# An FFT long-convolution layer and an MLP on one core: the second MLP weight loaded behind the first gate, unpadded tables in the first stage for ssm_k, and another order of GpSimd's first work

## The chip, the cores and the metric

The kernel runs on one core of a Trainium2 chip. The time is the device time of one execution in microseconds (us). The engines are TensorE (PE; its weight loads are shown as PEld), VectorE (DVE), ScalarE (ACT), GpSimd (POOL) and SyncE (SP), which here only issues transfers. ScalarE issues a few transfers as well. The core has 16 DMA engines.

## The reference

```python
# B, S, D, Dff, ks = 1, 2048, 512, 1376, 4; bf16 inputs
def _A_ref(q, k, v, shift_k, ssm_k, ssm_D):          # gated long convolution
    k_pad = jnp.pad(k, ((0, 0), (ks - 1, 0), (0, 0)))
    for t in range(ks):                              # 4 taps along the tokens
        k_shift = k_shift + k_pad[:, t:t + S, :] * shift_k[:, ks - 1 - t]
    kv = k_shift * v
    y_f = rfft(pad(kv, 2 * S)) * rfft(pad(ssm_k, 2 * S))     # along the tokens
    y = irfft(y_f)[:S].astype(bfloat16)
    y = y + kv * ssm_D
    return q * y

def _B_ref(x, w1, w2):                               # MLP
    h = jnp.maximum(jnp.einsum("bsd,df->bsf", x, w1), 0)
    return jnp.einsum("bsf,fd->bsd", h, w2)

x = A_q
h = x + _A_ref(_layernorm(x), A_k, A_v, A_shift_k, A_ssm_k, A_ssm_D)
return h + _B_ref(_layernorm(h), B_w1, B_w2)
```

## The kernel before

The order of every engine's instructions is the order in which the program writes them (`tc.manual_schedule()`); waits are put in by the framework where one instruction needs another's data or buffer. The program has two halves.

**The convolution.** The transform over the tokens is done as two stages of matmuls with tables of sines and cosines that the kernel makes itself. `to_rows` transposes `ssm_k` (tile `sk`) into `kfl` with 64 TensorE transposes. Then, in eight rounds `gb`, `taps` multiplies `k` by diagonal matrices `wdiag` (one block of four taps for each 128 channels, `rg` = 0 to 3; round `gb` uses blocks `2 * (gb % 2)` and the next) and VectorE multiplies by `v`; and `stage1(kfl, a1k, gb, ...)` does a part of the first stage for `ssm_k`. `stage1` has two forms. With `pairs=True` (only `gb == 2` for `kfl`) a matmul takes 64 rows and all 128 columns of the padded tables `f2hi`, `f2lo`. Otherwise it takes 32 rows and 64 columns. The table is kept as a high and a low bf16 part: `f1hi`, `f1lo` are 64 columns wide; `f2hi`, `f2lo` are 128 wide and hold in each block of 32 rows the same 64 columns, alternately left and right, with zeros beside them. GpSimd makes the `wdiag` blocks (L229), `f1hi` and `f1lo` (L231 to L233) and the padded copies (L237), then negated tables `c2n` (L240). The same `stage1` later works on `xfl`, the transform of `kv`. The second stage, the product of the two transforms and the first stage of the inverse (`inv1`) follow; the span is then at about 115 us.

**The gate and the MLP.** The 2048 tokens are four groups `q` of 512, each with two halves `h`. `lift(q)` transposes x into `xT[q]` and `ln1_norm(q)` normalises it and transposes it into `qT[q]`, both by DMA transposes on SyncE's queue. `inv2(q, h, ...)` is the last stage of the inverse transform: 64 matmuls with 32 rows each, into a PSUM tile `pz`. `gate(q, h)` on VectorE multiplies `pz` by `qT` (L602, which frees `pz`), adds `xT` (L605), and has SyncE transpose the result back to `xh` (L607). The pool `psz` has one `pz` buffer, so the next `inv2` from it waits for the L602 of the gate before it; `psz0` has a second one at the start only. `mlp1(sc)` makes the hidden layer of a group: 11 blocks `fc` of 4 matmuls with `w1`, each followed by a ReLU on ScalarE into `h1T`. `mlp2(sc)` has four blocks of 11 matmuls with `w2` (tile `w2`, shown as `w` in the profile, like `w1`), each followed by an addition on VectorE and the output's transfers. Hooks put further `half(q, h)` calls (an `inv2` and a `gate`) between these blocks: `half(1, 1)` behind the first block of `mlp2(0)`, `half(2, 0)` behind the third.

`w2` is loaded by `load_w2()`, two DMAs from ScalarE's queue (L681, 1280 KB, and L683, 96 KB). It is called in the hook of `mlp1(0)` at `fc == 1`, so ScalarE issues it behind its second ReLU. The tile lies in a pool that is opened at L593, after `inv1`.

The order at the start of the second half is: `inv2(0, 0)`, `inv2(0, 1)`, `gate(0, 0)`, `inv2(1, 0)`, `gate(0, 1)`, `lift(2)`, `ln1_norm(1)` (which makes `qT[1]`), the wrap of some table arguments, `ln1_stats(2)`, `gate(1, 0)`, `mlp1(0)`, `lift(3)`, `stats(xh[0])`, `ln1_norm(2)`, `mlp2(0)`.

Of the kernel before, what the change touches and what calls it, by code (L numbers as in the profile page):

```python
# [9 lines left out]
ALU = mybir.AluOpType  # L10
# [5 lines left out]
P = 128  # L16
# [40 lines left out]
def kernel(  # L57
# [13 lines left out]
    nc = tc.nc  # L71
    _, S, D = A_q.shape
    DFF = B_w1.shape[1]
# [114 lines left out]
    for a, t in cs:  # L188
        ks = slice(a, a + t.shape[1])
        nc.vector.tensor_tensor(out=tsn[:, ks, :], in0=ta[:, ks].unsqueeze(2).to_broadcast([P, t.shape[1], 64]),  # L190
                                in1=ta[:, 32:96].unsqueeze(1).to_broadcast([P, t.shape[1], 64]), op=ALU.add)
# [7 lines left out]
    f1f = early.tile([P, 64], F32, name="f1_f")  # L199
# [21 lines left out]
    f1hi = early.tile([P, 64], BF16, name="f1_hi")  # L221
    f1lo = early.tile([P, 64], BF16, name="f1_lo")
    f2hi = consts.tile([P, P], BF16, name="f2_hi")
    f2lo = consts.tile([P, P], BF16, name="f2_lo")
# [3 lines left out]
    for rg in range(DC):  # L228
        nc.gpsimd.tensor_tensor(out=wdiag[:, rg, :, :], in0=ident[:].unsqueeze(1).to_broadcast([P, KS, P]),  # L229
                                in1=wsh[:, rg, :].unsqueeze(2).to_broadcast([P, KS, P]), op=ALU.mult)  # L230
    nc.gpsimd.tensor_copy(out=f1hi[:, 0:64], in_=f1f[:])  # L231
    nc.gpsimd.tensor_tensor(out=f1f[:], in0=f1f[:], in1=f1hi[:, 0:64], op=ALU.subtract)
    nc.gpsimd.tensor_copy(out=f1lo[:, 0:64], in_=f1f[:])  # L233
    for f, g in ((f1hi, f2hi), (f1lo, f2lo)):
        for rg in range(DC):
            rows = slice(32 * rg, 32 * rg + 32)
# [1 line left out]
    for a, b in ((0, 8), (8, 16), (16, 22), (22, 24), (24, 32)):  # L238
        (ao, to), (ai, ti) = [[p for p in tab if p[0] <= a][-1] for tab in (cn, cs)]
        nc.gpsimd.tensor_single_scalar(out=to[:, a - ao:b - ao, :], in_=ti[:, a - ai:b - ai, :].bitcast(F32), scalar=-1.0,  # L240
                                       op=ALU.mult)

    def copy(eng, o, i):
        if eng == "A":
            nc.scalar.copy(out=o, in_=i)  # L245
        else:
            nc.vector.tensor_copy(out=o, in_=i)
# [9 lines left out]
    def bank2(name):  # L257
        return place([P, 2, 512], F32, name)
# [11 lines left out]
    def stage1(fl, a_out, gb, engs, pairs=False):  # L270

        pss = [bank2("ps1") for _ in range(2)]
        n, tabs = 2 if pairs else 4, (f2hi, f2lo)
        K = P // n
        for gi in range(8):
            for f in range(2):
                for t in range(n):
                    rows = slice(K * t, K * t + K)
                    cols = slice(0, P)
                    if pairs:  # L280
                        o = pss[t][:, gi // 4, 128 * (gi % 4):128 * (gi % 4) + 128]
                    else:
                        cols = slice(64 * (t % 2), 64 * (t % 2) + 64)
                        o = pss[t // 2][:, t % 2, 64 * gi:64 * gi + 64]
                    nc.tensor.matmul(out=o, lhsT=fl[rows, 8 * gb + gi, :, :].rearrange("p d n -> p (d n)"),  # L285
                                     rhs=tabs[f][rows, cols], start=(f == 0), stop=(f == 1),
                                     tile_position=(K * t, 0), skip_group_check=True)
        for h in range(2):
            if pairs:
                src = pss[h][:].rearrange("p b (g r c) -> p c (b g) r", g=4, r=2)  # L290
            else:
                src = pss[h][:].rearrange("p r (g c) -> p c g r", c=64)
            dst = a_out[:, :, 32 * gb:32 * gb + 32].rearrange("p c (g r) -> p c g r", r=DC)[:, :, :, 2 * h:2 * h + 2]
            for g, eng in enumerate(engs[h]):
                n = 8 // len(engs[h])
                copy(eng, dst[:, :, g * n:g * n + n], src[:, :, g * n:g * n + n])
# [12 lines left out]
    kfl = early.tile([P, 64, 2, 64], BF16, name="kfl")  # L309
# [26 lines left out]
    for gb in range(8):  # L336
        taps(gb // 2, gb % 2)
        stage1(kfl, a1k, gb, ("AA", "AD")[gb % 2], pairs=(gb == 2))
        if gb in (0, 1, 3, 5):
            cc_part()  # L340
# [21 lines left out]
    for q in range(8):  # L362
# [4 lines left out]
        if "DADDADAD"[q] == "D":  # L367
            nc.vector.tensor_single_scalar(out=xfl32[:, :, :, ms],
                                           in_=pst[:].bitcast(I32).rearrange("p m (d g) -> p g d m", d=2),
# [23 lines left out]
    for gb in range(8):  # L393
        stage1(xfl, a1x, gb, ("A", "DA" if gb == 4 else "D"), pairs=(gb > 0))
# [114 lines left out]
    def ec_sins(q):  # L509
        for h, t in ((0, ecs[q % 2]), (1, ecr[q % 2])):  # L510
            _sin(ecore[q][:, h, :, :].rearrange("p j n -> p (j n)"), t, 8192, neg=(h == 1))
# [83 lines left out]
    w2 = mp.tile([P, NFC, D], BF16, name="w2")  # L595
# [4 lines left out]
    def gate(q, h):  # L600
        ii = slice(2 * h, 2 * h + 2)
        nc.vector.tensor_tensor(out=qT[q][:, ii].rearrange("p i r t -> p r i t"),  # L602
                                in0=pzs[q, h].rearrange("p r (i a) n -> p r i (a n)", i=2),
                                in1=qT[q][:, ii].rearrange("p i r t -> p r i t"), op=ALU.mult)
        nc.vector.tensor_tensor(out=xT[q][:, ii], in0=qT[q][:, ii], in1=xT[q][:, ii], op=ALU.add)  # L605
        hT[q] = xT[q]
        nc.sync.dma_start_transpose(out=xh[q][:, ii].rearrange("p i (r c) -> p (i r) c", r=DC),  # L607
                                    in_=hT[q][:, ii].rearrange("p i r t -> p (i r) t"))

    def inv2(q, h, pool, width=4):  # L610
        pz = pool.tile([P, DC, 512], F32, tag="pz", name="pz")[:]
        pzs[q, h] = pz[:, :, 0:256].rearrange("p r (j n) -> p r j n", n=32)
        for jl in range(8):
            j = 8 * h + jl
            n2 = 16 * (j % 4) + 4 * q + j // 4
            w = min(width, 16 - j)
            for rho in range(2):
                for rg in range(DC):
                    rows = slice(32 * rg, 32 * rg + 32)
                    nc.tensor.matmul(out=pz[:, rg, 32 * jl:32 * (jl + w)],  # L620
                                     lhsT=ax[rows, 64 * rho + n2, :, :].rearrange("p d g -> p (d g)"),
                                     rhs=ecore[q][rows, rho, j:j + w, :].rearrange("p a b -> p (a b)"),
                                     start=(rho == 0), stop=(rho == 1), tile_position=(32 * rg, 0), skip_group_check=True)
# [40 lines left out]
    pl.pop("psIb")  # L664
    psz = pl.push("psZ", space=PSUM)
    psz0 = pl.push("psZ0", space=PSUM)
    inv2(0, 0, psz, 8)
    inv2(0, 1, psz0, 8)
    gate(0, 0)
    inv2(1, 0, psz, 8)  # L670
    gate(0, 1)
    pl.pop("psZ0")
# [3 lines left out]
        inv2(q, h, psz)  # L676
        gate(q, h)

    def load_w2():
        nfull = DFF // P  # L680
        nc.scalar.dma_start(out=w2[:, 0:nfull, :], in_=B_w2[0:nfull * P, :].rearrange("(c p) d -> p c d", p=P))  # L681
        if DFF % P:
            nc.scalar.dma_start(out=w2[0:DFF % P, nfull, :], in_=B_w2[nfull * P:DFF, :])  # L683

    def in_mlp1_0(fc):
        if fc == 1:
            load_w2()
        if fc in (6, 8):
            ec_sins(2 + (fc - 6) // 2)

# [18 lines left out]
    ln1_stats(2)  # L709
    gate(1, 0)  # L710
    mlp1(0, in_mlp1_0)
    lift(3)
    stats(xh[0], mv2, rstd2, 0)
# [44 lines left out]
```

## Time and profile before

| What | Value |
|---|---|
| time, median of 5 runs | 218.22 us (217.30 to 219.06) |
| time of the profiled execution | 217.86 us |
| its span | 216.1 us |
| mean granted TensorE clock | 0.991 |
| TensorE busy | 196.4 us, 91% of the span |
| VectorE, ScalarE, GpSimd busy | 144.3, 116.3, 79.1 us |
| w2's larger DMA (1280 KB), issue to landing | 9.9 us |
| w1's DMA (1376 KB), issue to landing | 6.0 us |

In the profile, times count from the start of the span. A line of the timeline gives start, duration, engine, source line, operation, output and inputs, the number of instructions, and in brackets how long the engine sat idle before it and what ended that. A line of the chain of waits gives start, duration and what was running, traced back from the last instruction. "Granted clock" is the share of full speed that TensorE's clock was given in a stretch. The profiled execution's own time is 1.8 us more than its span.

### The profile page before, as it was taken

What the parts mean: (1) busy time and instruction counts of PE and PEld (TensorE: products, weight loads), DVE (VectorE), ACT (ScalarE), POOL (GpSimd) and SP (SyncE); (2) the same over time, 40 slices, a digit from 0 to 9 for tenths busy, and PEclk for the clock granted to TensorE, in tenths of its full rate; (3) what the DMA queues carried; (4) which work ended last, traced back from release to release, by engine and by line L of the source; (5) the groups of instructions that cost most, each with busy time, mean ns of one, the idle gap of its engine ahead of it and who ended that gap; (6) DMA issues with size and microseconds to landing.
All of it is one profiled execution on the core that took longest, in us unless ns stands there. A gap on an engine that the chain in (4) does not pass through costs nothing.

```text
span 216.1 us, 5476 instructions
## 1 busy us (share of the span) xinstructions
PE 196.4 (91%) x2267; PEld 137.0 (63%) x2267; DVE 144.3 (67%) x238; ACT 116.3 (54%) x178; POOL 79.1 (37%) x120
## 2 busy tenths in 40 slices
PE   0399999999987999999998995999999999999992
PEld 0395546999766999979997642554646644444451
DVE  7997778766887998986969940987395470243031
ACT  2967988755894888886991275002450047016400
POOL 3299992000016999977678020010202010002000
PEclk9999999999999999999999998899999999999999
DMA  6999950000000017549630599494454430010012
GB/s 188 310 223 187 156 129 10 2 0 3 3 3 2 3 46 182 228 111 200 113 67 3 104 265 189 75 188 88 92 88 86 97 73 3 24 49 24 0 48 53
DMA packets 49513, 20.08 MB, mean 93 GB/s; under 512 B 44400, under 2 KB 47952, under 8 KB 49488
## 3 DMA queue, kind: packets, MB, share of 16 engines
q1 hardware_dynamic: 47360, 18.24, 40.6%
q10 hardware_dynamic: 2128, 1.48, 2.8%
q8 instruction: 18, 0.29, 0.5%
q14 instruction: 7, 0.06, 0.1%
HBM read 7.08 MB, written 2.10 MB: 42 GB/s over the span
## 4 chain that ended last, share of the span: by engine, by line
PE 75%; DMA 10%; DVE 8%; ACT 3%; issue 1%; SPq 0%; DVEq 0%; ACTq 0%
PE ps2m L649 19%; PE ps1m L632 14%; PE pkv L328 7%; PE psy L435 6%; DMA w<-in_B_w_dram 5%; PE pz L620 4%; PE ps L285 4%; DMA sk<-in_A_ssm_k_dram 4%; PE ps2k L303 3%; PE ps2k L305 3%; PE u L303 3%; PE pst L267 3%; PE u L305 3%; PE psi L562 3%; DVE st L515 2%; PE pst L365 2%
## 5 line engine op out<-in xcount | busy, mean ns | idle before, releaser
L634 ACT ACTIVATE h1T<-ps1m 128x512 bf16<-128x512 f32 (+1 forms) x44 | 25.8, 596 | 60.0 <-PE ps1m L632 59.9
L649 PE MATMUL ps2m<-w,h1T 128*128 128x512 bf16 (+3 forms) x187 | 41.1, 378 | 2.3 <-DMA w<-in_B_w_dram 2.3
L632 PE MATMUL ps1m<-xT,w 128*128 128x512 bf16 (+1 forms) x176 | 38.8, 379 | 0.4 <-DVE xT L605 0.4
L652 DVE SCALAR_TENSOR_TENSOR o<-ps2m,rstd,xh 128x512 bf16<-128x512 f32 (+1 forms) x17 | 12.1, 718 | 31.2 <-PE ps2m L649 29.0
L649 PEld LDWEIGHTS <-h1T 128*128 128x128 bf16 (+1 forms) x187 | 18.2, 100 | 23.0 <-DMA w<-in_B_w_dram 2.7
L632 PEld LDWEIGHTS <-w 128*128 128x128 bf16 (+1 forms) x176 | 17.4, 100 | 20.7 <-DVE xT L605 0.6
L425 POOL TENSOR_TENSOR t<-usb,kf 128x320 fp32r<-128x320 f32 x32 | 28.2, 945 | 2.4 <-ACT usb L421 2.1
L425 DVE TENSOR_TENSOR t<-u,kf 128x704 fp32r<-128x704 f32 x32 | 26.7, 889 | 3.4 <-ACT usb L421 3.4
L519 POOL TENSOR_SCALAR rstd<-mv 128x4 f32<-128x4 f32 x8 | 2.3, 283 | 71.5 <-DVE mv L517 71.5
L602 DVE TENSOR_TENSOR qT<-pz,qT 128x1024 bf16<-128x1024 f32 x8 | 9.7, 1218 | 15.0 <-DMA qT<-qln 8.4
L515 DVE BATCH_NORM_STATS2 st<-xh 128x6 f32<-128x512 bf16 x32 | 19.7, 677 | 0.0
L245 ACT CAST kf<-psy 128x512 fp32r<-128x512 f32 x30 | 17.6, 646 | 1.9 <-PE psy L435 0.2
L620 PEld LDWEIGHTS pz<-ecore,ax 32*128 32x128 f32 x512 | 15.0, 186 | 3.1 <-issue 1.3
L620 PE MATMUL pz<-ecore,ax 32*128 32x128 f32 (+7 forms) x512 | 15.7, 273 | 0.7 <-DVE wm L550 0.7
L435 PE MATMUL psy<-t,ipos 128*128 128x512 f32 x48 | 16.0, 394 | 0.0
L562 PE MATMUL psi<-dre,kf 128*128 128x256 f32 x64 | 15.5, 285 | 0.0
L562 PE MATMUL psi<-dim,kf 128*128 128x256 f32 x64 | 15.3, 281 | 0.0
L328 PE MATMUL pkv<-kT,wdiag 128*128 128x512 bf16 x64 | 15.2, 381 | 0.0
L267 PE MATMUL pst<-ident,sk 128*128 128x128 bf16 x64 | 6.7, 297 | 9.1 <-DMA sk<-in_A_ssm_k_dram 9.1
L331 DVE TENSOR_TENSOR sk<-pkv,vT 128x512 bf16<-128x512 f32 x16 | 10.9, 690 | 5.5 <-PE pkv L328 5.5
L245 ACT CAST a1k<-ps 128x1024 fp32r<-128x1024 f32 x12 | 12.6, 1093 | 3.4 <-PE ps L285 3.4
L245 ACT CAST ax<-psi 128x1024 fp32r<-128x1024 f32 x13 | 12.4, 1017 | 3.0 <-PE psi L562 2.9
(116 smaller groups left out, 389.2 us busy)
## 6 DMA issues: line engine op xcount, KB each, us to landing
sk<-in_A_ssm_k_dram SPq DMA_DIRECT2D x1, 2048.0 KB, 8.4
xh<-in_A_q_dram SPq DMA_DIRECT2D x16, 128.0 KB, 3.2
out_dram<-o SPq DMA_DIRECT2D x60, 32.0 KB, 1.6
w<-in_B_w_dram SPq DMA_DIRECT2D x1, 1376.0 KB, 6.0
w<-in_B_w_dram ACTq DMA_DIRECT2D x1, 1280.0 KB, 9.9
xh<-xT SPq DMA_TRANSPOSE x8, 3.1
w<-in_B_w_dram ACTq DMA_DIRECT2D x1, 96.0 KB, 9.8
kT<-in_A_k_dram SPq DMA_TRANSPOSE x4, 6.6
```

The costliest lines, as they stand in the source:

```text
L245: nc.scalar.copy(out=o, in_=i)
L267: nc.tensor.transpose(out=pst[:, i, :], in_=src[:, :, :, 8 * q + i], identity=ident[:])
L303: nc.tensor.matmul(out=ps[:, kk, :], lhsT=at_k1(w_re, k1), rhs=a_in[:, k1, :], start=True, stop=False, skip_group_check=True)
L328: nc.tensor.matmul(out=pss[i][:], lhsT=wdiag[:, 2 * h + i, j, :], rhs=kT[c][:, 2 * h + i, 16 - j:CH + 16 - j], start=(j == 0), stop=(j == ...
L425: eng.tensor_tensor(out=t[:, :, j, :], in0=in0.unsqueeze(1).to_broadcast([P, 2, n, 2]), in1=kfr[:, :, j, ks], op=ALU.mult)
L435: nc.tensor.matmul(out=psy[:], lhsT=m_[:], rhs=t_.rearrange("p j k -> p (j k)"), start=first, stop=not first)
L515: nc.vector.bn_stats(out=st[:, i, :], in_=src[:, i, :])
L562: nc.tensor.matmul(out=ps[:, i // 2, i % 2, :], lhsT=kf[:, c, 4 * m:4 * m + 4, :].rearrange("p r k -> p (r k)"), rhs=d[:].rearrange("p d a ...
L620: nc.tensor.matmul(out=pz[:, rg, 32 * jl:32 * (jl + w)], lhsT=ax[rows, 64 * rho + n2, :, :].rearrange("p d g -> p (d g)"), rhs=ecore[q][ro ...
L632: nc.tensor.matmul(out=ps1[:fsz, :].rearrange("p (i t) -> p i t", i=4), lhsT=w1[:, c, fc * P:fc * P + fsz], rhs=hT[sc][:, :, c, :], start= ...
L634: nc.scalar.activation(out=h1T[:fsz, fc, :], in_=ps1[:fsz, :], func=ACT.Relu)
L649: nc.tensor.matmul(out=ps2[:, 0:w], lhsT=h1T[:ksz, fc, i * P:(i + 1) * P], rhs=w2[:ksz, fc, ds], start=(fc == 0), stop=(fc == NFC - 1))
```

## The change

Three edits. First, GpSimd makes `f1hi` and `f1lo` after the second of the four `wdiag` blocks and not after the fourth. Second, `stage1` for `kfl` reads `f1hi` and `f1lo` in its form without pairs; the form with pairs, and both forms for `xfl`, read `f2hi` and `f2lo` as before. Third, `load_w2()` is called right behind `gate(0, 0)`, after a new VectorE memset of one column in each of `w2`'s 11 chunks (128 partitions x 11 elements). The load writes over that column, so its DMA waits for the memset, and the memset stands on VectorE behind the two operations of `gate(0, 0)` and ahead of those of `gate(0, 1)`. The call in the hook of `mlp1(0)` is gone.

```diff
     for rg in range(DC):
         nc.gpsimd.tensor_tensor(out=wdiag[:, rg, :, :], in0=ident[:].unsqueeze(1).to_broadcast([P, KS, P]),
                                 in1=wsh[:, rg, :].unsqueeze(2).to_broadcast([P, KS, P]), op=ALU.mult)
-    nc.gpsimd.tensor_copy(out=f1hi[:, 0:64], in_=f1f[:])
-    nc.gpsimd.tensor_tensor(out=f1f[:], in0=f1f[:], in1=f1hi[:, 0:64], op=ALU.subtract)
-    nc.gpsimd.tensor_copy(out=f1lo[:, 0:64], in_=f1f[:])
+        if rg == 1:
+            nc.gpsimd.tensor_copy(out=f1hi[:, 0:64], in_=f1f[:])
+            nc.gpsimd.tensor_tensor(out=f1f[:], in0=f1f[:], in1=f1hi[:, 0:64], op=ALU.subtract)
+            nc.gpsimd.tensor_copy(out=f1lo[:, 0:64], in_=f1f[:])
...
-        n, tabs = 2 if pairs else 4, (f2hi, f2lo)
+        n, tabs = 2 if pairs else 4, (f2hi, f2lo) if pairs or fl is not kfl else (f1hi, f1lo)
...
-                        cols = slice(64 * (t % 2), 64 * (t % 2) + 64)
+                        if fl is not kfl:
+                            cols = slice(64 * (t % 2), 64 * (t % 2) + 64)
+                        else:
+                            cols = slice(0, 64)
...
     inv2(0, 0, psz, 8)
     inv2(0, 1, psz0, 8)
     gate(0, 0)
+    nc.vector.memset(w2[:, :, 0:1], 0.0)
+    load_w2()
     inv2(1, 0, psz, 8)
     gate(0, 1)
...
     def in_mlp1_0(fc):
-        if fc == 1:
-            load_w2()
         if fc in (6, 8):
             ec_sins(2 + (fc - 6) // 2)
```

More of the change, by code (lines that the diff above doesn't have):

```diff
@@ L666, with load_w2 @@
     psz0 = pl.push("psZ0", space=PSUM)
+    def load_w2():
+        nfull = DFF // P
+        nc.scalar.dma_start(out=w2[:, 0:nfull, :], in_=B_w2[0:nfull * P, :].rearrange("(c p) d -> p c d", p=P))
+        if DFF % P:
+            nc.scalar.dma_start(out=w2[0:DFF % P, nfull, :], in_=B_w2[nfull * P:DFF, :])
     inv2(0, 0, psz, 8)
@@ L677, in half @@
         gate(q, h)
[L679 to L683, printed above, removed]
     def in_mlp1_0(fc):
-        if fc == 1:
-            load_w2()
         if fc in (6, 8):
```

## The prediction

> **What bounds the kernel now.** I read the page first: TensorE (PE) is busy for most of the span, so only its gaps can be won.
>
> ```profile
> span 216.1 us, 5476 instructions
> PE 196.4 (91%) x2267; PEld 137.0 (63%) x2267; DVE 144.3 (67%) x238; ACT 116.3 (54%) x178; POOL 79.1 (37%) x120
> ```
>
> Then the chain of waits in order of time, around the load that is moved:
>
> ```profile
> 120.75 0.70 DVE xT L605
> ...
> 121.50 1.91 PE ps1m L632 x8
> ...
> 123.44 9.95 DMA w<-in_B_w_dram
> ...
> 133.44 4.24 PE ps2m L649 x11
> 137.68 1.89 PE pz L620 x61
> ```
>
> The reader is to see that a transfer sits in the chain: w2 is asked for at 123.44, behind two ReLUs, lands 9.95 us later, and TensorE's first second-layer block (11 matmuls) starts at once. Third, the timeline of TensorE there:
>
> ```profile
> 121.50 9.67 PE L632 MATMUL ps1m<-xT,w 128*128 128x512 bf16 x44 [0.43 <-DVE xT L605]
> 133.44 4.24 PE L649 MATMUL ps2m<-w,h1T 128*128 128x512 bf16 x11 [2.27 <-DMA w<-in_B_w_dram]
> ...
> 146.30 2.55 PE L649 MATMUL ps2m<-w,h1T 128*128 128x512 bf16 x11
> ```
>
> The gap is 2.27 us, and the block behind it takes 4.24 us where the same 11 matmuls take 2.48 in the chain at 146.37. The table of stretches (TensorE busy, then its granted clock, DMA share, GB/s) says why:
>
> ```profile
> 61.96:65.37 3.41, 2.07 (x63) 1.00 0.00 0
> ...
> 130.23:133.64 3.41, 1.14 (x6) 1.00 1.19 165
> 133.64:137.05 3.41, 3.41 (x9) 0.50 0.32 72
> ```
>
> After a stretch of 3.41 us in which TensorE worked 1.14 us, it got half clock for the next 3.41 us. After one with 2.07 busy (1.35 idle) it did not. So w2's lateness costs 2.27 + (4.24 - 2.48) = 4.03 us. Fourth, who else waits on a transfer: the timeline of VectorE (DVE) and of SyncE's queue (SPq).
>
> ```profile
> 118.89 0.69 DVE L605 TENSOR_TENSOR xT<-qT,xT 128x1024 bf16<-128x1024 bf16 x1
> 119.50 1.22 DVE L602 TENSOR_TENSOR qT<-pz,qT 128x1024 bf16<-128x1024 f32 x1
> ...
> 135.18 1.23 DVE L602 TENSOR_TENSOR qT<-pz,qT 128x1024 bf16<-128x1024 f32 x1 [8.45 <-DMA qT<-qln]
> ```
>
> ```profile
> 119.61 3.09 SPq L607 DMA_TRANSPOSE xh<-xT  x2
> 122.81 1.90 SPq L523 DMA_TRANSPOSE xT<-xh  x1
> 124.80 7.38 SPq L523 DMA_TRANSPOSE qT<-qln  x1
> ```
>
> gate(1, 0) at 135.18 waits for the transpose qT[1], issued at 124.80 and landed 10.3 us later, at 135.1. inv2(1, 1) needs the PSUM tile that this gate frees at 135.18 + 1.23 = 136.41. Now that hides behind the slow block, which ends at 137.68. It is what is late next.
>
> **The change part by part.**
>
> *GpSimd's order and the unpadded tables.* No instruction is added. The first stage for ssm_k issues as many matmuls of 64 columns, on f1 instead of f2, and TensorE's order is the same.
>
> ```profile
> 9.44 4.91 POOL L229 TENSOR_TENSOR wdiag<-ident,wsh 128x512 bf16<-128x512 bf16 x4 [6.27 <-DMA wsh<-in_A_shift_k_dram]
> ...
> 16.32 1.09 POOL L237 COPY f_lo<-f_lo 32x64 bf16<-32x64 bf16 x4
> ```
>
> The padded copies end at 16.32 + 1.09 = 17.41. TensorE's first stage-1 matmul is at 17.50, straight behind its taps (chain: 15.84 + 1.73 = 17.57), so it waits for nothing. After: two wdiag blocks end near 9.44 + 4.91/2 = 11.9 (f1's sines end at 10.41), hi and lo take 0.94 (14.29 to 15.23 now) to 12.85, the other two wdiag blocks end near 15.3 and are first needed at 18.11: 2.8 us of cover. The padded tables still end at 17.4, but are first needed at the paired third block, at 22.40. Value taken: 0. A later wsh could make it a gain of a few tenths in a run; a loss needs 2.8 us.
>
> *The memset.* One DVE instruction more, 128x11, between gate(0, 0) and gate(0, 1). This trace has none of its strided form; its nearest rows are memsets of 0.06 us (128x1) and 0.09 us (128x32). I take 0.1, ends 0.05 and 0.2. It is on the path: mlp1(0) starts when gate(0, 1) ends, so TensorE ends mlp1(0) at 131.17 + 0.1 = 131.27.
>
> *The load's two issues* leave ScalarE (ACT) behind the second ReLU (0.38 + 0.97 us) and run near 119.7 to 121.1, when the memset has ended. ScalarE is idle from 114.99 to 122.58, so the wait added on its queue delays only what starts at 122.58: nothing. The last ReLU of mlp1(0), at 132.7 because two pairs of sines of 1.3 us come before it, is needed by the block's eleventh matmul, at 131.27 + 10 x 0.216 = 133.4.
>
> *The load itself* starts 3.7 us earlier. From issue to landing it took 9.95 us among transposes; w1, of the same 1376 KB, took 6.0 us without company. So it lands between 125.7 and 129.7, and is needed at 131.27: 1.5 us of cover even at the worse end. The block then ends at 131.27 + 2.48 = 133.75 instead of 137.68. Were this all, the gain is 3.9 us.
>
> *What the load is moved past:* on the 16 DMA engines, most of the first xh transpose, the second, xT[2] and qT[1]. They take turns with it packet for packet (queue 10 is w2's, queue 1 the transposes'):
>
> ```profile
> q10 hardware_dynamic: 271, 0.28, 79.8%
> q1 hardware_dynamic: 270, 0.07, 31.3%
> ```
>
> That is the microsecond from 126; alone, queue 1 moved 808 packets from 121 to 122. So the xh and xT[2] transposes come later, but their readers have room (stats of xh[0] at 137.05, gate(2, 0) at 146.4). qT[1] is last in queue 1 before and after, so it lands when the same total work is done. Only empty time can be saved: 0.4 us at 122.3 to 122.6 with nothing queued, which w2 now fills, and two stalls with work queued, 0.45 us at 129.1 to 129.6 and 1.2 us from 130.75:
>
> ```profile
> DMA packets 18, 0.01 MB, mean 11 GB/s; under 512 B 9, under 2 KB 18, under 8 KB 18
> ```
>
> (the microsecond from 131). The long stall follows an instruction fetch (queue 8) that runs from 129.98 on; the fetch at 20.04 was followed by the same dip, 36 packets in 0.6 us from 21.4. It may well return. So qT[1] lands between 135.1 - 0.4 - 1.65 = 133.1 (no stall) and 134.7 (both). I take 134.0, near the middle.
>
> *Sum.* inv2(1, 1) starts at landing + 0.05 + 1.23 + 0.05 = landing + 1.33: 135.35 instead of 137.68, a gain of 2.3 with TensorE idle for 135.35 - 133.75 = 1.6 us. The next place, inv2(2, 0), needs gate(1, 1), which VectorE frees 143.22 - 135.13 = 8.1 us after the landing; TensorE is there at landing + 1.33 + 1.89 + 4.86 = 8.08: no more than 0.1 lost. Behind it TensorE is the bound again. Total -2.2. The profiled execution (span 216.1, time 217.86, so 1.8 lies around the span) would be 215.7. The median of the runs is 0.36 higher at 218.22: 216.0.
>
> *A rule against the row.* The half clock after 1.14 busy in 3.41 us is weighed against the Trainium skill, "TensorE: Matmul & The Clock Gate", section "Why this matters for your kernels": it asks for no idle gaps above about 3 us, since a whole idle window is what drops the clock. By that rule 2.27 us would cost only itself, removing it while adding 1.6 would be worth 2.27 - 1.6 - 0.1 = 0.6 us, and the new gap could not cost clock. This trace shows the drop after 2.27 us of idling inside one stretch, so I use 4.03. By the trace the new gap has a price as well: idling above a point between 1.35 and 2.27 us in a stretch (1.8 by the middle) costs another 1.75 us.
>
> **The rivals.**
> - *Full gain:* both stalls vanish and qT[1] lands by 132.4. For: the last packets move faster once w2 is out of the way (867 packets from 133 to 134 against 541 at 126). Against: the total work. 218.2 - 3.9 = 214.3.
> - *The new wait turns cold:* qT[1] lands at 134.2 to 135.1; TensorE idles 1.8 to 2.7 us and may get half clock. With the drop: 136.35 - 134.7 - 1.75 = -0.1, so about 218.2; without it 216.6. For: the long stall can return. Against: the stretches run on a fixed grid, which may split the gap.
> - *Slower:* taking turns with w2 from the start makes queue 1 so late that qT[1] lands after 135.7, when the clock loss exceeds what is left of the gain by over 1.1 us. At 136.2: 136.35 - 136.2 - 1.75 = -1.6, so 219.8. For: turns cost queue 1 two thirds of its rate for about 5 us. Against: it gets that back when w2 is done.
> - *Nothing:* w2 does not start earlier, or the wait is exchanged one for one: 218.2. Against: ScalarE is idle at 119.7.
>
> **How the numbers follow.** A warm gap of up to 1.8 us, gain 2.1 to 3.9: 0.50; full gain 0.12; the later landing 0.23 (0.10 warm, 0.13 cold); slower by more than 1.1 us 0.08; nothing 0.07. About 0.5% (1.1 us) is what a measurement here can tell from no change. Faster: 0.50 + 0.12 + 0.10 = 0.72; same: 0.13 + 0.07 = 0.20; slower: 0.08. The range goes from 213.9 (full gain, with 0.4 for the front and for the run) to 218.5 (cold, plus 0.3); the warm case alone would be 214.3 to 216.2.
>
> **What would show it.** Right: w2 issued near 119.7 and landed before 130; ps2m behind ps1m without a gap; its 11 matmuls in 2.5 us; then a wait of inv2(1, 1) of about 1.6 us for gate(1, 0), which itself waits for qT. The front's rows up to 17.5 unchanged. Wrong: qT landed after 134.7 or half clock behind the new gap; TensorE waiting for wdiag at 18.1; or w2 landing after 131.

## The result and the profile after

The changed kernel runs in 217.02 us (median of 20 runs, 215.39 to 219.32) against 218.31 us for the one before (39 runs, 216.41 to 221.33). The ratio is 0.9925, with a 95% interval of 0.9901 to 0.995: about 1.6 us faster (1.1 to 2.2). Four of the 20 runs, at 219 us and with a mean granted clock of 0.979 to 0.984, lie over 1.5% above the fastest and are left out of the ratio; the median of the other 16 is 216.7 us, and no trace shows one of the four. The profiled execution took 217.20 us with a span of 215.4 us; before it was 217.86 and 216.1.

The chain of waits around the load now reads (start, duration, what was running):

```profile
121.86 6.23 PE ps1m L636 x28
...
128.85 5.05 DMA qT<-qln
...
133.99 1.24 DVE qT L606
135.22 0.04 issue
135.27 2.21 PE pz L624 x60
137.48 6.25 PE ps2m L653 x22
```

w2 has left the chain and the transpose qT[1] has taken its place: it lands at 133.90, VectorE's gate(1, 0) starts at 133.99, and inv2(1, 1) follows. TensorE's timeline shows what that leaves:

```profile
121.86 9.67 PE L636 MATMUL ps1m<-xT,w 128*128 128x512 bf16 x44 [0.44 <-DVE xT L609]
131.37 2.54 PE L653 MATMUL ps2m<-w,h1T 128*128 128x512 bf16 x11
135.27 2.21 PE L624 MATMUL pz<-ecore,ax 32*128 32x128 f32 x64 [1.36 <-DVE qT L606]
137.41 6.31 PE L653 MATMUL ps2m<-w,h1T 128*128 128x512 bf16 x22
143.65 2.01 PE L624 MATMUL pz<-ecore,ax 32*128 32x128 f32 x64
```

The first block follows mlp1(0) without a gap and takes 2.54 us (4.24 before). inv2(1, 1) waits 1.36 us and starts 2.34 us earlier than before (135.27 against 137.61). But the next 22 matmuls take 6.31 us; before, the same 22 took 4.93. So inv2(2, 0), at 143.65, is only 0.71 us earlier (144.36 before), and that is what is left at the end of the span. The lines of before for this are:

```profile
137.61 1.96 PE L620 MATMUL pz<-ecore,ax 32*128 32x128 f32 x64
139.50 4.93 PE L649 MATMUL ps2m<-w,h1T 128*128 128x512 bf16 x22
144.36 2.01 PE L620 MATMUL pz<-ecore,ax 32*128 32x128 f32 x64
```

The table of stretches in after (TensorE busy, granted clock, DMA share, GB/s) gives the reason:

```profile
65.16:68.57 3.41, 2.30 (x18) 1.00 0.01 2
...
133.42:136.84 3.42, 2.06 (x59) 1.00 0.00 0
136.84:140.25 3.41, 3.41 (x23) 0.50 0.98 181
```

The stretch with the new gap has 2.06 us of work, and the next stretch got half clock. One with 2.30 did not lead to it. The half clock moved with the gap: from behind w2's wait to behind qT[1]'s.

The DMA queues also show that the load and the transposes did not share as expected. SyncE issued the two xh transposes at 119.96 and 121.8, ScalarE issued w2 at 120.03. The packets from 121 to 123 (queue 10 is w2's):

```profile
DMA packets 309, 0.32 MB, mean 158 GB/s; under 512 B 0, under 2 KB 309, under 8 KB 309
...
q10 hardware_dynamic: 309, 0.32, 52.1%
...
xh<-xT SPq DMA_TRANSPOSE x2, 7.3
```

Only w2's queue moved anything; the transposes' first packet went at 123.3, 3.4 us after the issue, where in before it went after 1.2 us. The second transpose landed 7.3 us after its issue (the landing of the first is not recorded; in `w2_only`, below, the two took 8.4 and 7.3 us), where they took 3.1 and 3.3 before. In the microsecond from 130, with nothing but qT[1] left, the stall came back:

```profile
DMA packets 41, 0.01 MB, mean 10 GB/s; under 512 B 41, under 2 KB 41, under 8 KB 41
```

An instruction fetch stands in the row of the microsecond before it (queue 8, one packet), as in the trace of before.

### The profile page after: what moved, and what is told of

It reads as the page before. It is cut to its first block, busy times and chain, and to the rows that moved or that the text cites. A ratio compares the mean times of both kernels' runs of the same rounds, so it can differ in the third digit from the quotient of the medians.

```text
span 215.4 us, 5479 instructions
## 1 busy us (share of the span) xinstructions
PE 196.2 (91%) x2267; PEld 137.2 (64%) x2267; DVE 144.4 (67%) x239; ACT 116.5 (54%) x178; POOL 79.2 (37%) x120
## 4 chain that ended last, share of the span: by engine, by line
PE 79%; DVE 8%; DMA 6%; ACT 4%; issue 2%; SPq 0%; DVEq 0%; ACTq 0%
PE ps2m L653 17%; PE ps1m L636 16%; PE psy L439 7%; PE pkv L332 7%; PE pz L624 5%; PE ps L289 4%; DMA sk<-in_A_ssm_k_dram 4%; PE ps2k L307 3%; PE ps2k L309 3%; PE u L307 3%; PE psi L566 3%; PE pst L268 3%; PE u L309 3%; DMA qT<-qln 2%; PE pst L369 2%; ACT ax L246 2%
```

## The experiments

The theory after the result: the gain comes from the load alone; what is missing of the full 3.9 us is the wait for qT[1] and, in part of the runs, the half clock behind it. Four kernels were run first, with 29 runs of before (median 218.52 us).

**The front alone.** The `f1hi` and `f1lo` edits stay, `load_w2()` is back in its hook.

```diff
-    nc.vector.memset(w2[:, :, 0:1], 0.0)
-    load_w2()
...
     def in_mlp1_0(fc):
+        if fc == 1:
+            load_w2()
```

> The two edits of the front alone; w2 loaded where it was. My theory: the time of before, 218.3 us within 0.3, since TensorE waited for no table at 17.5 us; the profile should still show the 2.27 us gap ahead of ps2m and half clock behind it. Rival: the front is worth something of its own. In the profile of after, TensorE's third block of stage 1 (at 22.4 us) took 1.63 us with a gap of 0.43 in it against 1.02 before, so the front could cost 0.3 us; or save as much.

Measured: 218.68 us, ratio 0.9993 (0.9954 to 1.0032). So no effect of the front is seen, but one of a few tenths of a us, as the rival had it, is within the interval (from 1.0 us faster to 0.7 us slower). Its profile has w2's gap, here 3.01 us long, since w2 landed 10.7 us after its issue (9.9 in before):

```profile
134.09 0.55 PE L653 MATMUL ps2m<-w,h1T 128*128 128x512 bf16 x1 [3.01 <-DMA w<-in_B_w_dram]
```

The gap of 0.43 us in the third block, seen in the profile of after, is not the front's either: a kernel with the old front (`before_qt_first`, below) has one of 0.79 us there, and `front_only` has none. Over all ten traces mlp1(0) starts at 121.40 to 122.83 us with the new front and at 121.50 to 122.75 with the old one.

**The load alone.** The other half of the change, on before's front.

> The earlier load of w2 alone, tables and GpSimd's order as before. My theory: all of the gain, 0.9925 of before or about 216.7 us, with the gap of about 1.4 us ahead of inv2(1, 1) and, in part of the runs, half clock behind it. Rival: the gain needs the front too, then about half of it.

Measured: 217.44 us, ratio 0.9947 (0.9912 to 0.9982). That interval holds the whole change's 0.9925, but also the rival's half of the gain (0.9963), so the times alone do not settle the shares. The traces do: w2's gap goes with this edit, and stays without it. The profiled execution has the same wait as after, and here no half clock behind it: 21 recorded matmuls in 4.93 us.

```profile
131.58 2.54 PE L649 MATMUL ps2m<-w,h1T 128*128 128x512 bf16 x10
135.54 1.96 PE L620 MATMUL pz<-ecore,ax 32*128 32x128 f32 x64 [1.42 <-DVE qT L602]
137.44 4.93 PE L649 MATMUL ps2m<-w,h1T 128*128 128x512 bf16 x21
```

The span of that execution is 214.4 us, a microsecond below after's. So the same gap costs clock in one execution and not in another. The stretches show more. In after's trace the clock fell at 136.84 and again behind the last matmul, at 215.34, and in before's at 133.64 and 215.56; the distances are 23 and 24 times 3.413 us, so the stretches lie on a grid, which can be counted back from that last fall. In `w2_only` the last fall is at 214.47, and the stretch with the gap is this one:

```profile
132.55:135.96 3.41, 1.99 (x24) 1.00 0.42 94
```

Its gap of 1.42 us lies whole in one stretch with 1.99 us of work, less than the 2.06 of after, and the clock stayed full.

**qT[1] ahead of xT[2], in after and in before.** One swap:

```diff
-    lift(2)
     ln1_norm(1)
+    lift(2)
```

> After, with lift(2) put behind ln1_norm(1), so that the transpose qT[1] goes ahead of xT[2] in SyncE's queue. My theory: what is left of the cost is that qT[1] lands at 133.9 behind xT[2]; 2048 packets fewer ahead of it let it land near 131.5, so TensorE has no gap ahead of inv2(1, 1) and keeps its clock: about 1.4 + 1.7 us less than the profiled after, 214.3 us (0.981 of before). Rival: VectorE's chain behind gate(1, 0) or xT[2] is late next and takes the place: then 215.5 to 217, no better than the good runs of after.

> The same swap in before. My theory: nothing, 218.3 us within 0.3: w2 sets the block's start there, and qT[1] is hidden behind it. Rival: the order of the transposes is worth something by itself, 1 us or more.

Measured: on after 214.38 us (214.00 to 214.83), ratio 0.9807 (0.9768 to 0.9846); on before 218.52 us, ratio 0.9989 (0.9953 to 1.0024). The swap is worth nothing while w2 is late, and about 2.3 us (216.7 - 214.4, from two sets of runs) once it is early. Timeline of VectorE and TensorE with the swap on after:

```profile
131.74 1.22 DVE L606 TENSOR_TENSOR qT<-pz,qT 128x1024 bf16<-128x1024 f32 x1 [5.08 <-DMA qT<-qln]
```

```profile
130.93 2.54 PE L653 MATMUL ps2m<-w,h1T 128*128 128x512 bf16 x10
133.40 1.96 PE L624 MATMUL pz<-ecore,ax 32*128 32x128 f32 x64
135.30 4.93 PE L653 MATMUL ps2m<-w,h1T 128*128 128x512 bf16 x21
```

gate(1, 0) starts at 131.74 and TensorE has no gap. The rival, that VectorE's chain or xT[2] is late next, is out.

The swap on before shows a third case of the clock. w2's gap is 2.08 us there, and no half clock follows (stretch counted back from the last fall at 216.30):

```profile
122.75 9.67 PE L632 MATMUL ps1m<-xT,w 128*128 128x512 bf16 x44 [0.43 <-DVE xT L605]
134.50 2.55 PE L649 MATMUL ps2m<-w,h1T 128*128 128x512 bf16 x10 [2.08 <-DMA w<-in_B_w_dram]
...
130.96:134.37 3.41, 1.46 (x7) 1.00 1.24 182
```

Four more kernels ran together with 11 runs of before (median 219.72 us), and after was not among them. Their ratios lean on a before that is 1.2 us slower in the median than in the first set, in its runs of low clock: 7 of 11 at 0.992 or less (median 220.0), where the first set has 14 of 27 (218.9). Those with a mean granted clock of 0.995 or more agree (217.9 us here, 218.1 there). So times are compared here, across the sets.

**The gap filled, the wait kept.** Six matmuls whose result nobody reads:

```diff
         if i == 0:
+            keep = psm.tile([P, 512], F32, tag="ps", name="keep")
+            for _ in range(6):
+                nc.tensor.matmul(out=keep[:].rearrange("p (i t) -> p i t", i=4), lhsT=w1[:, 0, 0:P],
+                                 rhs=hT[0][:, :, 0, :], start=True, stop=True)
             half(1, 1)
```

> After, with six matmuls more (1.3 us) whose result nobody reads, put between the first block of mlp2(0) and inv2(1, 1), where TensorE waits for gate(1, 0). The wait for qT[1] stays, the idle time goes. My theory: the slower half of the runs of after (217.2 us) has half clock behind that gap and the faster half (215.8 us) has not; so the filler costs nothing and brings all runs to about 215.8 us, with no stretch of half clock behind it. Rival: the spread comes from elsewhere (the front, DMA stalls), or the clock counts something that the filler does not feed; then 217.0 us or more, or the filler's own 1.3 us on top: 218.3.

Measured: 216.07 us (215.92 to 216.46), ratio 0.9864 (0.982 to 0.9908).

```profile
134.01 1.23 DVE L606 TENSOR_TENSOR qT<-pz,qT 128x1024 bf16<-128x1024 f32 x1 [6.93 <-DMA qT<-qln]
```

```profile
133.73 1.46 PE L699 MATMUL keep<-xT,w 128*128 128x512 bf16 x6
135.29 1.96 PE L624 MATMUL pz<-ecore,ax 32*128 32x128 f32 x64
137.18 4.93 PE L653 MATMUL ps2m<-w,h1T 128*128 128x512 bf16 x21
```

qT[1] is as late as in after and inv2(1, 1) starts as late (135.29 against 135.27), but the matmuls behind it run at full clock in the profile, and all six runs lie within 0.6 us. This separates the two costs. The 16 runs of after that count fall into eight with a mean granted clock of 0.991 or 0.992 (median 217.2) and eight with 0.998 or more (median 215.8); one stretch of half clock is 0.5 x 3.41 us of a span of 215.4, or 0.008. The filler's 216.1 is near the second group, and useless work alone brought the median down by 0.6 us (216.7 - 216.1). In all 30 runs of the five kernels whose gap is filled or gone, this one, the swap on after and the three below, the mean granted clock is 0.995 or more; with the gap it is 0.992 or less in 8 of after's 16 and in 6 of `w2_only`'s 12. The swap's 214.4 is then 1.4 us below after's group at full clock, which is the gap itself.

**The blocks moved instead.** half(1, 1) and half(2, 0) stand one block later; the transfers are those of after.

```diff
-        if i == 0:
+        if i == 1:
             half(1, 1)
-        if i == 2:
+        if i == 3:
             half(2, 0)
```

> After, with half(1, 1) and half(2, 0) behind the second and fourth block of mlp2(0) in place of the first and third. The transfers stay as they are; TensorE has 2.5 us more work of its own ahead of inv2(1, 1). My theory: the gap of 1.4 us and the half clock both go, so 214.3 to 214.8 us, as when qT[1] goes first. Rival: gate(1, 1) and gate(2, 0) come later and mlp1(1) or mlp2(1) waits for them: 215.5 to 217.

Measured: 214.76 us (214.33 to 215.19), ratio 0.9802 (0.9758 to 0.9846). gate(1, 0) starts at 133.75, as late as in after, and costs nothing because TensorE has a block of its own to do. So the late transfer was harmful only through the order of TensorE's work.

**The load before the gates.** `load_w2()` (its definition moves up too) right behind the tile's line, without the memset, alone and with the swap.

```diff
     w2 = mp.tile([P, NFC, D], BF16, name="w2")
+    load_w2()
...
     gate(0, 0)
-    nc.vector.memset(w2[:, :, 0:1], 0.0)
-    load_w2()
```

> After, with w2's load issued as soon as its tile exists (ScalarE issues it behind its last copy of ax, at about 115.3 us, while the DMA engines are idle), without the memset; the transposes keep their order. My theory: w2 lands by about 122 and queue 1 has the engines to itself, so qT[1] lands near 131 and TensorE has no gap: 214.3 us, like qT[1] first. Rival: qT[1] is late because of the stall behind the instruction fetch at about 130 and of xT[2] ahead of it, not because of w2; then it lands near 133 and 1 us of the gap stays: 215.5 us.

> Both: w2 as soon as its tile exists, and qT[1] ahead of xT[2]. My theory: nothing is left to win behind either one, 214.3 us within 0.3. Rival: each covers a part, and both together are 0.5 us or more below qT[1] first alone.

Measured: 214.50 us (214.07 to 215.12), ratio 0.9795 (0.9746 to 0.9843), and with the swap 214.61 us (214.36 to 215.06), ratio 0.9799 (0.9755 to 0.9842). With w2 out of the way before the transposes, they keep their order and gate(1, 0) is still early enough:

```profile
131.18 1.23 DVE L613 TENSOR_TENSOR qT<-pz,qT 128x1024 bf16<-128x1024 f32 x1 [4.01 <-DMA qT<-qln]
```

The two ways do not add up: they remove the same wait. These four gapless kernels, at 214.4 to 214.8 us, beat both kernels.

## Why the prediction was right, and where its size was off

- *The front, valued at 0:* right within what the runs resolve (0.9993, 0.9954 to 1.0032).
- *w2's load:* right. Issued at 120.03 (said: near 119.7), landed 7.6 us later, at 127.6 (said: 125.7 to 129.7), needed at 131.4. The block behind it took 2.54 us (2.48).
- *The memset:* it took 0.07 us (0.1) and is recorded beside the gate's operation, from 119.93. gate(0, 1) starts 1.85 us after gate(0, 0), against 1.83 before, so it cost about 0.02.
- *qT[1] as the next thing late:* right, and to the tenth: landing 133.90 (said 134.0), inv2(1, 1) at 135.27 (135.35), TensorE idle 1.36 us (1.6). But the tenth is luck, because the reason given for it failed. The prediction said that the transfers do the same total work and that only empty time can be saved. The two queues moved the same 7680 packets, in before from 120.78 to 134.60 with about 2.0 us empty, in after from 121.13 to 133.46 with about 2.2 us empty: two stalls stood there again (0.3 us from 127.0, 1.2 us from 129.7), and 0.7 us behind w2's first packets was empty too. With both stalls the prediction's sum gives 134.7. What fell is the time in which packets moved, from about 11.8 to 10.1 us. The transpose xT[2], alone on the DMA engines in one microsecond of before (from 124) and one of after (from 128):

```profile
q1 hardware_dynamic: 715, 0.18, 103.5%
...
q1 hardware_dynamic: 1131, 0.28, 125.5%
```

  Why it is faster in after is open. The prediction also let the first transposes take turns with w2 from the start, while they moved nothing before 123.
- *The step that was mis-sized is the clock.* The prediction took idle time in a stretch as what decides, set the point at 1.8 us, the middle of 1.35 and 2.27, and so forecast a gap at full clock and -2.2 us. In the profiled execution of after 1.36 us of idling was enough: 6.31 us against 4.93 for 22 matmuls, and 2.21 against 1.96 for inv2(1, 1), or 1.6 us. That the profiled after gains only 0.7 us is this one term: 2.3 less 1.6. And there is no such point in idle time: 1.95 us in the stretch of `before_qt_first` and 1.42 in that of `w2_only` cost no clock. About half of the counted runs of after have the lower clock, and the measured gain is 1.6 us; its interval just reaches 2.2. The group at full clock, at 215.8 us, is what was forecast (216.0).
- *The price of the gap in before* was taken from one execution (2.27 + 1.76). In `before_qt_first`, w2's gap of 2.08 us had no half clock behind it in the profiled execution (its first block took 2.55 us). So 1.76 is what it costs when it falls badly, not always, and the runs of before spread as after's do: of 27 counted in the first set, 14 had a mean granted clock up to 0.992 (median 218.9 us) and 13 had 0.995 or more (218.1). Between runs of the same clock the gain from before to after is thus 1.7 us (218.9 to 217.2) or 2.2 (218.1 to 215.8), while the two profiled gaps differ by only 0.9 (2.27 and 1.36). The rest is open. The gap of the late load may often be longer than in the one profile of before, which is about 1 us below its group's median: it was 2.08, 2.27 and 3.01 us in three profiles.
- *The rule of the Trainium skill* ("TensorE: Matmul & The Clock Gate", section "Why this matters for your kernels") on gaps above about 3 us would have given 0.6 us. The measured 1.6 lies between that and the trace's 2.2. The rule's price of nothing for a gap of 1.4 us is refuted by after's half clock and by the filler.
- *The full-gain rival* needed qT[1] by 132.4. It did not happen in after, and it is what the swap brought (214.38; said 214.3). The slower rival needed a landing after 135.7.

The stall behind the instruction fetch was not tried: what is shown is that it follows the fetch in the traces of before and after, not that the fetch causes it.

## What to carry to other kernels

Before moving a late transfer, write down the next wait behind it, and which transfers it pushes back: here a load that was issued 3.4 us earlier gave 1.6 us, and one swap among the transposes that it pushed back gave 2.3 more. Where TensorE must wait, move work of its own into the gap, because a short wait can cost as much again in clock. And read a clock penalty from more than one execution: a time that comes in two groups, with two values of the mean granted clock, tells more than a single profile.

## What the runs showed of the hardware

- Neither the length of a gap nor the busy time of its stretch of 3.41 us tells whether half clock follows. What the other work in the stretch is fits all five profiled gaps (us of TensorE work in the stretch):

| Execution | Idle | Matmuls with 128 rows | inv2, 32 rows | Next stretch |
|---|---|---|---|---|
| `before_qt_first` | 1.95 | 1.46 | 0 | full clock |
| `w2_only` | 1.42 | 1.57 | 0.42 | full clock |
| after | 1.36 | 0.49 | 1.57 | half clock |
| before | 2.27 | 1.14 | 0 | half clock |
| `front_only` | 3.01 | 0.40 | 0 | half clock |

  So matmuls with 32 rows seem to count for less. They do count: 2.88 us of them and 0.09 of the others kept the clock in a stretch of `after_half_later`, from 118.27. If a weighted sum decides, 1 us of inv2 counts as about 0.4 to 0.6 us of the wide matmuls, an estimate from these rows ((1.14 - 0.09) / 2.88 and (1.46 - 0.49) / 1.57). No kernel was run to test it. Where the grid falls relative to the gap differs from execution to execution, which would explain why after has two groups of runs.
- The first DMA transpose, issued 0.07 us ahead of a 1280 KB load from another queue, moved no packet before 123.3, 3.4 us after its issue, while the load's packets went out from 121.1; in before, without the load, its first packet went 1.2 us after the issue. Landing took 7.3 us for the second transpose, 3.1 and 3.3 us for the two in before. With the load out of the way they took 3.8 and 3.3 us again (`w2_at_pool`). Why the load goes first is open.
